# The floor of a decay scan moved into the scan, and its minimum gathered by ScalarE and taken once

## The chip, the core and the metric

The kernel runs on one core of a Trainium2 chip. A core has TensorE (PE: matrix products and transposes, with a separate track for weight loads, PEld), VectorE (DVE), ScalarE (ACT), GpSimd (POOL) and SyncE (SP, which here issues most DMAs). Each engine works through its own queue in order and waits on semaphores for what others write. The metric is the device time of the program in microseconds; smaller is better. All data is float32.

## What is computed

A gated linear recurrence (attention without softmax) for 4 batches, 8 heads, 768 positions and head width 48, then a SwiGLU block on the 3072 x 384 result:

```python
f = 1.0 / (1.0 + np.exp(-f_logit))
for t in range(S):
    state = f[:, :, t, :, None] * state + np.einsum('bhd,bhe->bhde', k[:, :, t], v[:, :, t])
    y[:, :, t] = np.einsum('bhd,bhde->bhe', q[:, :, t], state)
x = y.transpose(0, 2, 1, 3).reshape(B * S, H * D)
g = x @ w_gate
out = (g * (1.0 / (1.0 + np.exp(-g))) * (x @ w_val)) @ w_out
```

`q`, `k`, `v` and `f_logit` are (4, 8, 768, 48); `w_gate` and `w_val` are 384 x 1536, `w_out` is 1536 x 384. The entries of `f_logit` are drawn around 2.0 with a deviation of 0.5.

## The kernel before

**Chunks and units.** The sequence is cut into 6 chunks of 128 positions. A unit is one chunk `c` of one batch `b`, numbered `u = 4 * c + b`, so there are 24 units, 0 to 23. Within a unit the 8 heads lie as 4 pairs: partitions 0 to 47 and 64 to 111 hold the 48 channels of the two heads of a pair, and the free axis holds 4 pairs times 129 positions (one position ahead of each chunk, `N1 = C + 1`), 516 elements.

**What a unit does** (`attention`, a generator whose `yield`s let other work be put between its steps). Its gates come through a sigmoid on ScalarE into `gate` (by PE transposes in chunks 0 and 1, L563, by a VectorE transpose of 32 x 32 squares later, L566). A first scan on VectorE (L577) runs backward over the positions and forms `tail`, the product of the gates behind each position. Element 1 of each pair's row is then the product over the whole chunk, `whole`. Three small VectorE instructions follow, each on 128 x 4 elements: `least` is updated with the minimum of itself and `whole` (L580); `start` gets the larger of `whole` and `LEAST = 2^-60` (L581); `start` becomes its reciprocal (L582). The keys are multiplied by `tail` (`kT`, L587). A second scan (L601) runs forward from `start`, which gives the inverse products that the queries are multiplied with (`qT`, L607). TensorE forms the scores of 8 heads from `kT` and `qT` (L620) and, in most units, turns `kT` back (L624); ScalarE copies that to `kt` (L631), and VectorE applies the causal mask to the scores (`A`, L633). `decayed` is the old state times `whole` (L541). Then come the outputs `y` (L654 to L694) and the new state (`dS`, L699, L706, L708).

**The short path and the check on it.** The division by `whole` is sound only if no product over a chunk falls below `LEAST`. So the whole computation above is a short path, and `judge` looks at `least` once, near the end: a minimum over its elements on VectorE (L1317), a transpose on TensorE (L1320), a minimum over the partitions that hold channels (L1322), and a comparison with `LEAST` (L1324). The flag is loaded into registers (L1326), and only where it is set is a general path run after it (L1331). `judge` runs in the last chunk's block of the second part, after the last unit's scans.

**Staging and order.** Chunk 0's four units come first, woven together by hand. Then chunk 0's SwiGLU is done in a plain form (`mlp_plain`) together with chunk 1's units (32 to about 148 us in the profile), while the weights, which arrive as pairs of 32-bit words, are put together by ScalarE (`up`, `top`: L462, L464) and VectorE (L470 to L476). From chunk 1's SwiGLU on, the products with the three weights use schemes with fewer multiplications and more additions (`mlp_fifteen`, `down_seven`): TensorE's products (L959, L1058, L1121) are copied out by ScalarE (`c`, `aside`: L964) or added by VectorE (L860, L863), followed by silu on ScalarE (L975) and a product on VectorE (L911). The units of chunks 2 to 5 are put between these products at times written out as a table (`CHAINS`, `SCORES`, `times`).

For chunk 0 with the start of chunk 1, and for everything from about 148 us on, the order of each engine's instructions is fixed as the program writes it (`in_order`, L1226 and L1288). Between them, in the stretch of `mlp_plain`, the order is left to the scheduler of the language, but for the sums of weights.

**Buffers.** Chunks 0 and 1 alternate between two tiles `gates0/1` and two `tails0/1`; later chunks all use `gates0` and `tails0`, so a unit's first scan writes the tile that the unit before it has read. `ones` is a constant tile, 1 at the first position of each pair's row and 0 elsewhere: as the scan's second operand it starts each pair's product anew. Its memory, read as bfloat16, also feeds a few idle matmuls at the start (`keep_warm`). `least` is one 128 x 4 tile, filled with 1.0 at the start (L370).

Of the kernel before, what the change touches and what calls it, by code (L numbers as in the profile page):

```python
# [9 lines left out]
FP32 = mybir.dt.float32  # L10
# [3 lines left out]
ALU = mybir.AluOpType  # L14

LEAST = 2.0 ** -60
# [273 lines left out]
def short_path(ctx, tc, ident, least, judge, q, k, v, f_logit, moe_w_gate, moe_w_val, moe_w_out, out):  # L290
# [9 lines left out]
    nc = tc.nc  # L300
# [3 lines left out]
    HP = H // 2  # L304
# [6 lines left out]
    N1 = C + 1  # L311
# [6 lines left out]
    const = ctx.enter_context(tc.tile_pool(name="const", bufs=1))  # L318
# [29 lines left out]
    tails = [(first_pool if i else const).tile([128, HP * N1 + 2], FP32, tag=f"tails{i}", name=f"tails{i}")  # L348
             for i in range(NROT)]
    start = const.tile([128, HP * N1], FP32, tag="start", name="start")  # L350
    ones = const.tile([128, HP * N1], FP32, tag="ones", name="ones")
    nc.vector.memset(ones, 0.0)
    nc.vector.memset(ones.rearrange("p (a t) -> p a t", t=N1)[:, :, 0:1], 1.0)

    def keep_warm(n):


        p = fps.tile([128, 512], FP32, tag="m", name="idle")
        some = ones.bitcast(mybir.dt.bfloat16)
        for _ in range(n):  # L360
            nc.tensor.matmul(p, lhsT=some[:, 0:128], rhs=some[:, 0:512], start=True, stop=True)

    def pairs(t, off=0):
        return t[:, off:off + HP * N1].rearrange("p (a t) -> p a t", t=N1)
# [2 lines left out]
        nc.vector.memset(t, 0.0)  # L367
    for t in tails:
        nc.vector.memset(t, 1.0)
    nc.vector.memset(least, 1.0)  # L370

    spare = const.tile([128, 1], FP32, tag="spare", name="spare")
    nc.gpsimd.memset(spare, 0.0)
# [144 lines left out]
    def bank(name):  # L518
        return banks[-1].tile([128, 512], FP32, tag="a", name=name)
# [10 lines left out]
    def attention(u):  # L530
# [3 lines left out]
        gate, tail = (x[u % NROT if c < SQUARES else 0] for x in (gates, tails))  # L534
# [14 lines left out]
        def transposed(name, src):  # L549
            p = bank(name)  # L550
            for a in range(HP):
                nc.tensor.transpose(p[:, a * C:(a + 1) * C],
                                    src[:, 2 * a:2 * a + 2, :].rearrange("t r d -> t (r d)"), ident)
            return p.rearrange("p (a t) -> p a t", t=C)
# [6 lines left out]
        else:  # L561
            p = transposed("fTp", fr)
# [9 lines left out]
        if c >= SQUARES:  # L572
# [1 line left out]
        yield  # L574

        n = HP * N1
        nc.vector.tensor_tensor_scan(tail[:, 0:n][:, ::-1], gate[:, 0:n][:, ::-1], ones[:, ::-1], 1.0,  # L577
                                     op0=ALU.mult, op1=ALU.add)
        whole = pairs(tail)[:, :, 1:2]
        nc.vector.tensor_tensor(least, least, whole.rearrange("p a t -> p (a t)"), ALU.min)  # L580
        nc.vector.tensor_single_scalar(pairs(start)[:, :, 0:1], whole, LEAST, op=ALU.max)  # L581
        nc.vector.reciprocal(pairs(start)[:, :, 0:1], pairs(start)[:, :, 0:1])  # L582
        yield
        if c < SQUARES:
            kp = transposed("kTp", kr)
# [35 lines left out]
        if c < NCH - 1 and not turned:  # L621
            p = bank("kt")
            for a in range(HP):
                nc.tensor.transpose(p[:, a * C:(a + 1) * C], kT[:, a, :], ident)  # L624
        yield
        if c < NCH - 1:
            kt = att.tile([128, HP * C], FP32, tag="kt", name="kt")
            if turned:
                nc.sync.dma_start(out=kt, in_=turn.rearrange("t i a r e -> i t (a r e)"))
            else:  # L630
                nc.scalar.copy(kt, p)  # L631
# [10 lines left out]
        if c and b < B - 1:  # L642
# [8 lines left out]
            for a in range(HP):  # L651
                for par in range(2):
                    r = rows_of(par)
                    nc.tensor.matmul(place(a, par), lhsT=decayed[r, a, :], rhs=qT[r, a, :],  # L654
                                     start=a < 2, stop=False, skip_group_check=True)
            for par in range(2):
                for a in range(HP):
                    nc.tensor.matmul(place(a, par), lhsT=v_[:, 2 * a + par, :], rhs=A[:, par, a, :],  # L658
                                     start=False, stop=a >= HP - 2, skip_group_check=True)
# [3 lines left out]
            for h in range(H):  # L663
                a, par = h // 2, h % 2
                f = h * D
                while f < (h + 1) * D:
                    n = min((h + 1) * D, (f // 128 + 1) * 128) - f
# [28 lines left out]
        if c < NCH - 1:  # L696
            p = bank("dS")
# [19 lines left out]
    def attention_steps(c):  # L717

        runs = [attention(c * B + b) for b in range(B)]
        parts = [3, 6, 3, 3]  # L720
        order = sorted((2 * b + s, b, n) for b in range(B) for s, n in enumerate(parts))
        return [lambda b=b, n=n: [next(runs[b]) for _ in range(n)] for _, b, n in order]
# [104 lines left out]
    whole = NJ * TRIPLE + 7 * DOWN  # L827
# [339 lines left out]
    load(0, "v")  # L1167
    mark = traced[-1]
    keep_warm(5)
    first = [attention(b) for b in range(B)]  # L1170
    done = [0] * B

# [18 lines left out]
    for b in range(1, B):  # L1191
        if b == 1:
            run(1, 0)
            keep_warm(6)
        run(b, 1)
        run(b - 1, 3)
        run(b, 2)
        load_ahead(b)
        if b + 1 < B:
            run(b + 1, 0)  # L1200
        else:
            sizes.pop(0)()
        run(b - 1, 4)
# [51 lines left out]
    for c in range(2, NCH):  # L1255
        for b in range(B):
            run = attention(c * B + b)
            waiting += [((c - 2) * whole + t, lambda run=run: next(run)) for t in times(c)[b]]
# [32 lines left out]
@with_exitstack  # L1291
def kernel(
    ctx: ExitStack,
    tc: tile.TileContext,
    q: bass.AP,
    k: bass.AP,
    v: bass.AP,
    f_logit: bass.AP,
    moe_w_gate: bass.AP,
    moe_w_val: bass.AP,  # L1300
    moe_w_out: bass.AP,
    out: bass.AP,
):


    nc = tc.nc
    args = (q, k, v, f_logit, moe_w_gate, moe_w_val, moe_w_out, out)
    HP, D = q.shape[1] // 2, q.shape[3]
    flags = ctx.enter_context(tc.tile_pool(name="flags", bufs=1))
    least = flags.tile([128, HP], FP32, tag="least", name="least")  # L1310
    ident = flags.tile([128, 128], FP32, tag="idf", name="idf")
    make_identity(nc, ident)
    redo = []

    def judge(bank):
        low = flags.tile([128, 1], FP32, tag="low", name="low")
        nc.vector.tensor_reduce(low, least, axis=mybir.AxisListType.X, op=ALU.min)  # L1317
        yield
        row = bank("row")[0:1, 0:128]
        nc.tensor.transpose(row, low, ident)  # L1320
        one = flags.tile([1, 1], FP32, tag="one", name="one")
        nc.vector.tensor_reduce(one, row.rearrange("p (n d) -> p n d", n=2)[:, :, 0:D], axis=mybir.AxisListType.XY, op=ALU.min)  # L1322
        flag = flags.tile([1, 1], I32, tag="flag", name="flag")
        nc.vector.tensor_single_scalar(flag, one, LEAST, op=ALU.is_lt)  # L1324
        yield
        redo.append(nc.values_load(flag[0:1, 0:1], min_val=0, max_val=1,  # L1326
                                   skip_runtime_bounds_check_because="a comparison"))
        yield

    short_path(tc, ident, least, judge, *args)  # L1330
    with tc.If(redo[0] > 0):  # L1331
        general_path(tc, *args)
# [32 lines left out]
```

## Time and profile before

| | |
|---|---|
| device time, median of 3 runs | 612.46 us (612.24 to 613.02) |
| the profiled execution | its span, first to last instruction: 611.2 us; the page gives no time beside it |
| TensorE clock granted | 0.999 of full, mean |
| the chain that ended last, by engine | PE 67%, DVE 9%, DMA 3%, issue 3%, ACT 3%, SP queue 2% |
| first scan, L577 | 24 x 1.23 us |
| minimum, L580; maximum, L581; reciprocal, L582 | 24 each, 0.165, 0.165 and 0.180 us |
| second scan, L601 | 24 x 1.23 us |
| copies of 128 x 512 on ScalarE, L631 | 14 x 0.586 us |
| minimum in `judge`, L1317 | 0.15 us, at 536.7 us |

The profile is one execution's. A line of the page's groups or of the timeline names the source line, the engine, the operation, what is written and read, shape and count, and the busy time. A bracket at the end of a timeline line gives the idle time of the engine just before the instruction and what ended it. Durations of neighbours on VectorE and ScalarE overlap[...]. The distance between two starts therefore says better than the duration what an instruction holds its engine for.

### The profile page before, as it was taken

How to read it: one execution, taken by the hardware profiler on the slowest of the kernel's cores; microseconds unless marked ns; L12 is line 12 of the kernel's file. 1: busy time of each engine (PE TensorE's matmuls, PEld its weight loads, DVE VectorE, ACT ScalarE, POOL GpSimd, SP SyncE). 2: the span in 40 equal slices, each digit the busy share in tenths (PEclk: the TensorE clock that was granted, in tenths of full speed). 3: DMA queues.
4: the chain of work that ended last, by engine and by line, in shares of the span. 5: the costliest groups of instructions: out<-in, count | busy, mean ns of one | idle time of the engine just before them, and what ended most of it. 6: DMA issues, size and time to landing. Idle time of an engine off the chain costs nothing.

```text
span 611.2 us, 10816 instructions
## 1 busy us (share of the span) xinstructions
PE 594.2 (97%) x4036; PEld 487.9 (80%) x4036; DVE 499.2 (82%) x882; ACT 286.7 (47%) x530; POOL 7.6 (1%) x52
## 2 busy tenths in 40 slices
PE   7799999999999999999999999999999999999996
PEld 4654545566888799888899988899988899988896
DVE  7999989878999996999996889996879991566731
ACT  2465646313776522476732366742276730366600
POOL 1000000000000000000000000000000000000000
PEclk9999999999999999999999999999999999999999
DMA  9999582005323134424235344145313100100001
GB/s 149 249 213 284 174 250 79 1 14 154 89 52 69 27 95 113 118 54 96 53 95 122 104 111 111 31 114 118 105 51 90 27 6 10 53 1 2 0 1 58
DMA packets 109143, 54.10 MB, mean 89 GB/s; under 512 B 68761, under 2 KB 102169, under 8 KB 109081
## 3 DMA queue, kind: packets, MB, share of 16 engines
q1 hardware_dynamic: 107064, 50.56, 34.6%
q10 hardware_dynamic: 2016, 2.75, 1.2%
q8 instruction: 34, 0.56, 0.4%
q14 instruction: 29, 0.23, 0.1%
HBM read 44.04 MB, written 6.29 MB: 82 GB/s over the span
## 4 chain that ended last, share of the span: by engine, by line
PE 67%; DVE 9%; DMA 3%; issue 3%; ACT 3%; SPq 2%; ACTq 0%; POOL 0%; DVEq 0%; POOLq 0%
PE o L1058 15%; PE A L959 14%; PE B L959 11%; PE o L959 5%; PE o L780 5%; PE c L959 5%; PE o L1121 3%; PE sc L620 3%; PE y L658 2%; SPq L669 1%; DVE c L863 1%; PE y L679 1%; PE y L654 1%; PE dS L699 1%; DMA xT<-yT 1%
## 5 line engine op out<-in xcount | busy, mean ns | idle before, releaser
L1058 PE MATMUL o<-w_out,h 128*128 128x192 f32 x360 | 62.0, 327 | 0.5 <-DVE h L911 0.5
L959 PE MATMUL A<-xs,w_both 128*128 128x256 f32 x240 | 62.1, 381 | 0.0
L1058 PEld LDWEIGHTS o<-w_out,h 128*128 128x128 f32 x360 | 58.7, 190 | 1.7 <-DVE h L911 0.8
L964 ACT COPY c<-A 128x512 f32<-128x512 f32 x40 | 23.4, 584 | 61.3 <-PE A L959 61.3
L959 PEld LDWEIGHTS A<-xs,w_both 128*128 128x128 f32 x240 | 44.9, 190 | 6.5
L860 DVE TENSOR_TENSOR c<-c,aside 128x512 f32<-128x512 f32 x60 | 41.7, 694 | 9.8 <-ACT aside L964 8.4
L964 ACT COPY aside<-A 128x512 f32<-128x512 f32 x60 | 35.1, 586 | 30.9 <-PE A L959 30.9
L911 DVE TENSOR_TENSOR h<-h,c 128x256 f32<-128x256 f32 x100 | 41.3, 422 | 6.9 <-ACT h L975 6.8
L975 ACT ACTIVATE h<-c 128x256 f32<-128x256 f32 x100 | 39.4, 418 | 9.5 <-DVE c L860 5.8
L863 DVE TENSOR_TENSOR c<-c,aside 128x512 f32<-128x512 f32 x60 | 41.5, 692 | 2.0 <-ACT aside L964 1.7
L959 PE MATMUL B<-xs,w_both 128*128 128x256 f32 x160 | 41.2, 380 | 0.8 <-ACT aside L964 0.8
L1058 PE MATMUL o<-ws,h 128*128 128x192 f32 x240 | 41.5, 328 | 0.2 <-DVE A L633 0.2
L959 PE MATMUL c<-xT,w_both 128*128 128x256 f32 x160 | 41.2, 380 | 0.5 <-DVE c L863 0.5
L959 PE MATMUL A<-xs,extra 128*128 128x256 f32 x160 | 41.2, 380 | 0.0
L959 PE MATMUL B<-xT,extra 128*128 128x256 f32 x160 | 41.1, 379 | 0.0
L964 ACT COPY aside<-B 128x512 f32<-128x512 f32 x60 | 35.1, 586 | 11.4 <-PE B L959 6.9
L1058 PEld LDWEIGHTS o<-ws,h 128*128 128x128 f32 x240 | 39.1, 190 | 0.8 <-DVE A L633 0.4
L633 DVE TENSOR_TENSOR A<-sc,causal 128x512 f32<-128x512 f32 x48 | 30.8, 684 | 9.9 <-PE sc L620 9.8
L863 DVE TENSOR_TENSOR c<-o,c 128x512 f32<-128x512 f32 x40 | 27.8, 694 | 10.3 <-ACT h L975 5.8
L959 PEld LDWEIGHTS B<-xs,w_both 128*128 128x128 f32 x160 | 30.2, 190 | 5.2 <-ACT aside L964 1.2
L959 PEld LDWEIGHTS c<-xT,w_both 128*128 128x128 f32 x160 | 30.3, 190 | 5.0 <-DVE c L863 0.9
L959 PEld LDWEIGHTS A<-xs,extra 128*128 128x128 f32 x160 | 30.3, 190 | 4.4 <-ACT c L964 0.3
(140 smaller groups left out, 1138.8 us busy)
## 6 DMA issues: line engine op xcount, KB each, us to landing
fsquares<-in_f_logit_dram SPq DMA_DIRECT2D x64, 96.0 KB, 2.7
ksquares<-in_k_dram SPq DMA_DIRECT2D x64, 96.0 KB, 2.6
qsquares<-in_q_dram SPq DMA_DIRECT2D x64, 96.0 KB, 2.3
v<-in_v_dram SPq DMA_DIRECT2D x24, 192.0 KB, 3.2
w<-in_moe_w_gate_dram SPq DMA_DIRECT2D x6, 768.0 KB, 6.4
w<-in_moe_w_val_dram SPq DMA_DIRECT2D x6, 768.0 KB, 5.3
w<-in_moe_w_out_dram SPq DMA_DIRECT2D x6, 768.0 KB, 5.7
out_dram<-ob ACTq DMA_DIRECT2D x14, 192.0 KB, 2.3
```

What stands on the lines that cost most here:

```text
L620: nc.tensor.matmul(sc[par][:, a * C:(a + 1) * C], lhsT=kT[r, a, :], rhs=qT[r, a, :], start=True, stop=True)
L633: nc.vector.tensor_tensor(A[:, par], sc[par].rearrange("p (a t) -> p a t", t=C), causal.unsqueeze(1).broadcast_to((128, HP, C)), ALU.mult)
L658: nc.tensor.matmul(place(a, par), lhsT=v_[:, 2 * a + par, :], rhs=A[:, par, a, :], start=False, stop=a >= HP - 2, skip_group_check=True)
L780: nc.tensor.matmul(p, lhsT=hidden_tile(h, n // 2)[:, n % 2 * 2 + b // 2, b % 2 * C:(b % 2 + 1) * C], rhs=w_out[:, j, :], start=(n == 0), s ...
L860: nc.vector.tensor_tensor(dst, a, b, ALU.add)
L863: nc.vector.tensor_tensor(dst, a, b, ALU.subtract)
L911: lagging.append(lambda: f(*args))
L959: nc.tensor.matmul(p[name][:, n, :], lhsT=weights_of[a][:, n, j, :], rhs=tokens[b], start=fresh and n == 0, stop=True, skip_group_check=True)
L964: nc.scalar.copy(t, p[name])
L975: nc.scalar.activation(dst, src[:, 0, :], AF.Silu)
L1058: nc.tensor.matmul(p[:, n, :], lhsT=lhsTs[j][:, n * C:(n + 1) * C], rhs=rhs[:, j, :], start=first and j == order[0] and n == 0, stop=j == ...
L1121: nc.tensor.matmul(p, lhsT=hidden_tile(h, j)[:, 2, n * C:(n + 1) * C], rhs=b22[:, j, :], start=j == order[0], stop=j == order[-1])
```

## The change

The first scan's second operation becomes a maximum, and its second operand a tile `floor` that holds 1 at the first position of each pair's row and `LEAST` elsewhere. The gate at a pair's first position is 0, so the running value there becomes 1 as before; elsewhere a running product below `LEAST` is lifted to it. `whole` is then at least `LEAST`, and the separate maximum goes: the reciprocal is taken of `whole` directly. The running minimum goes as well. In its place ScalarE copies each unit's `whole` to a row of a larger `least` (24 rows of 4), in the step that follows the scores, ahead of the copy of `kt`. `judge` takes one minimum over all 96 elements of a partition, and its comparison becomes "at most `LEAST`", since a lifted product now equals it. The fill of `least` with 1.0 is dropped, as each row is written.

```diff
     start = const.tile([128, HP * N1], FP32, tag="start", name="start")
-    ones = const.tile([128, HP * N1], FP32, tag="ones", name="ones")
-    nc.vector.memset(ones, 0.0)
-    nc.vector.memset(ones.rearrange("p (a t) -> p a t", t=N1)[:, :, 0:1], 1.0)
+    floor = const.tile([128, HP * N1], FP32, tag="floor", name="floor")
+    nc.vector.memset(floor, LEAST)
+    nc.vector.memset(floor.rearrange("p (a t) -> p a t", t=N1)[:, :, 0:1], 1.0)
...
-        some = ones.bitcast(mybir.dt.bfloat16)
+        some = floor.bitcast(mybir.dt.bfloat16)
...
-    nc.vector.memset(least, 1.0)
...
         n = HP * N1
-        nc.vector.tensor_tensor_scan(tail[:, 0:n][:, ::-1], gate[:, 0:n][:, ::-1], ones[:, ::-1], 1.0,
-                                     op0=ALU.mult, op1=ALU.add)
+        nc.vector.tensor_tensor_scan(tail[:, 0:n][:, ::-1], gate[:, 0:n][:, ::-1], floor[:, ::-1], 1.0,
+                                     op0=ALU.mult, op1=ALU.max)
         whole = pairs(tail)[:, :, 1:2]
-        nc.vector.tensor_tensor(least, least, whole.rearrange("p a t -> p (a t)"), ALU.min)
-        nc.vector.tensor_single_scalar(pairs(start)[:, :, 0:1], whole, LEAST, op=ALU.max)
-        nc.vector.reciprocal(pairs(start)[:, :, 0:1], pairs(start)[:, :, 0:1])
+        nc.vector.reciprocal(pairs(start)[:, :, 0:1], whole)
         yield
...
         yield
+        nc.scalar.copy(least[:, u, :], whole.rearrange("p a t -> p (a t)"))
         if c < NCH - 1:
             kt = att.tile([128, HP * C], FP32, tag="kt", name="kt")
...
-    least = flags.tile([128, HP], FP32, tag="least", name="least")
+    least = flags.tile([128, q.shape[0] * q.shape[2] // 128, HP], FP32, tag="least", name="least")
...
-        nc.vector.tensor_reduce(low, least, axis=mybir.AxisListType.X, op=ALU.min)
+        nc.vector.tensor_reduce(low, least, axis=mybir.AxisListType.XY, op=ALU.min)
...
-        nc.vector.tensor_single_scalar(flag, one, LEAST, op=ALU.is_lt)
+        nc.vector.tensor_single_scalar(flag, one, LEAST, op=ALU.is_le)
```

## The prediction

> **What bounds the kernel now.** I read the page's first part, then the waits of TensorE by stretch, then the VectorE and ScalarE timelines around the lines that the change touches, and last the chain that ended last.
>
> ```profile
> PE 594.2 (97%) x4036; PEld 487.9 (80%) x4036; DVE 499.2 (82%) x882; ACT 286.7 (47%) x530; POOL 7.6 (1%) x52
> ```
>
> TensorE is busy for 97% of the span, so what VectorE saves is worth only what TensorE waits for VectorE. The waits of TensorE from 32 to 242 us, as the waits view has them (who waited for whom, total, times, longest):
>
> ```profile
> PE B L959 <- ACT aside L964: 0.8, 1, 0.8
> PE o L780 <- DVE h L771: 0.7, 1, 0.7
> PE o L1058 <- DVE h L911: 0.5, 1, 0.5
> PE c L959 <- DVE c L863: 0.5, 1, 0.5
> PE sc L620 <- DVE qT L607: 0.4, 1, 0.4
> PE o L1058 <- DVE A L633: 0.2, 1, 0.2
> ```
>
> These sum to 3.1 us. The same view from 242 to 606 us names no wait at all, and by stretch (PE busy, PEld busy, DVE busy, ...):
>
> ```profile
> 242.00:340.00 98.00, 97.91 (x729) 87.83 (x729) 86.61 (x153) 48.95 (x94) 0.84 (x5) 1.00 0.38 92
> 340.00:432.00 92.00, 92.00 (x682) 82.48 (x681) 80.11 (x142) 46.97 (x90) 0.84 (x5) 1.00 0.38 94
> 432.00:526.00 94.00, 94.00 (x632) 84.27 (x631) 71.80 (x132) 43.05 (x85) 0.74 (x4) 1.00 0.18 49
> ```
>
> There VectorE has gaps and TensorE none: units 12 to 23 (half of all) can give nothing. What one unit's first scan and the three small instructions behind it take, in the VectorE timeline (start, duration):
>
> ```profile
> 5.99 1.23 DVE L577 TENSOR_TENSOR_SCAN tails<-gates,ones 128x516 f32<-128x516 f32 x1 [1.77 <-ACT gates L563]
> 7.26 0.17 DVE L580 TENSOR_TENSOR least<-least,tails 128x4 f32<-128x4 f32 x1
> 7.34 0.16 DVE L581 TENSOR_SCALAR start<-tails 128x4 f32<-128x4 f32 x1
> 7.54 0.18 DVE L582 RECIPROCAL start<-start 128x4 f32<-128x4 f32 x1
> 7.63 0.66 DVE L587 TENSOR_TENSOR kT<-kTp,tails 128x512 f32<-128x512 f32 x1
> ```
>
> The minimum holds the engine for 0.08 us, since the independent maximum starts that much later; the reciprocal needs the maximum and starts 0.20 us behind it. With both gone the reciprocal can start at 7.26, so 0.28 us go per unit. Where other work was put between them (the fifth unit, at 43.92) less goes:
>
> ```profile
> 45.51 0.16 DVE L580 TENSOR_TENSOR least<-least,tails 128x4 f32<-128x4 f32 x1
> 45.59 0.17 DVE L581 TENSOR_SCALAR start<-tails 128x4 f32<-128x4 f32 x1
> 45.66 0.68 DVE L771 TENSOR_TENSOR h<-h,val 128x512 f32<-128x512 f32 x1
> ```
>
> Here the pair costs 0.15 us.
>
> [...] a scan of 516 elements takes 1228 ns (L577) where a plain two-operand instruction on 512 takes 681 (L633). [...] The nearest row here:
>
> ```profile
> L560 ACT ACTIVATE spare<-spare 128x1 f32<-128x1 f32 x4 | 0.8, 204 | 0.0
> ```
>
> So 0.20 us for the new 128x4 copy. The 128x512 copies (0.59 us) follow each other at 0.48 us, an overlap of 0.11, so the copy should hold ScalarE for about 0.09 us (estimate). [...] the page of the kernel has table loads only at L557, L560, L563, L767 and L975 (sigmoid and silu), so I charge no load.
>
> **The change part by part.**
>
> Scan with maximum in place of addition, 24 times. The trace doesn't show this form. [...] I take 1.23, unchanged[...].
>
> Minimum and maximum removed, 24 of each. On VectorE: 24 x 0.28 = 6.7 us at most. What of it reaches the end:
> - Units 0 to 3 (0 to 32 us): nothing. TensorE waits at 20.35 us for the load of the fourth fraw, which comes through a queue that is issuing without a pause from 0.8 us; the earlier savings end there. From there the path runs PE y, dS, sc, then VectorE's mask at 23.73 us, which itself waited 0.29 us for PE sc, so that unit 3's saving turns into a longer wait. Behind the mask no removed instruction stands.
> - Units 4 to 7 (32 to 148 us): VectorE is busy 43.3 of 46 us and then 60.2 of 70, alternating with ScalarE over the weight pieces. Unit 4's 0.15 comes off the 0.4 us wait of sc at 49.34. Unit 6's 0.14 (95.91 to 96.05) comes off the 0.7 us wait at 108.96, since VectorE has no gap from 90.98 to there. Unit 5's 0.15 I count as lost in the ScalarE waits at 76.93, 83.16 and 90.98. Unit 7's 0.14 works on sc at 128.16, which the chain shows starting 0.12 us after qT released it: 0.1.
> - Units 8 to 11 (148 to 242 us): unit 8's 0.28 works on sc at 160.09, released by qT as well: about 0.2, what the spacing of TensorE's starts is above usual there. Unit 9's is lost at 179.17, where VectorE waits 0.79 us for PE sc. Unit 10's (186.79) counts in full, because VectorE has no gap from 181 to 209 us and the waits at 194.43, 201.21 and 210.76 are its lag: 0.28. Unit 11's scan is at 219.08, behind the last such wait but the 0.2 of L633, which itself waits for TensorE: nothing.
> Sum: 0.15 + 0.14 + 0.1 + 0.2 + 0.28 = 0.87 us.
>
> The copy on ScalarE, 24 x 0.09 = 2.2 us of an engine with 47% work. It stands directly ahead of the kt copy of L631, or of the next thing where there is none. For units 0 to 3 ScalarE idles 3.13, 1.96, 1.40 and 1.40 us just there: hidden. For unit 9 there is no cover:
>
> ```profile
> 180.63 0.59 ACT L964 COPY c<-A 128x512 f32<-128x512 f32 x1 [2.41 <-PE A L959]
> 181.11 0.59 ACT L631 COPY kt<-kt 128x512 f32<-128x512 f32 x1
> 181.59 0.61 ACT L964 COPY c<-B 128x512 f32<-128x512 f32 x1
> ```
>
> Behind them are a table load and the silu of 183.51 (ends 183.93), and VectorE's L911 takes that at 184.00. 0.09 later makes VectorE lose some 0.06 in its stretch without gaps. From 242 us on no TensorE instruction waits, so a copy shifted by 0.09 is covered by the gaps of ScalarE. Charge: 0.1 us. Bounds: 0, and 8 units x 0.20 = 1.6 if the overlap failed and nothing hid it before 242 us.
>
> The new waits. The copy waits for the scan, which in the fixed order lies several VectorE instructions back. The next scan into the same tail waits for the copy; queued behind it on VectorE are the reciprocal, the kT product and all later additions. The closest pair is unit 8's copy at about 164.95 (ends 165.15) and unit 9's scan at 166.59: 1.4 us of cover; unit 12 to 13 has 2.3 us. Nothing.
>
> Judging once over 128x96 in place of 128x4: 0.15 us plus 92 x 1.02 ns (from (681 - 165) / 508) is 0.24, once, at 536.7 us, where TensorE doesn't wait. The last copy comes before the mask of unit 23 at 502 us. The memsets: the new fill is the old one with another value, one of 0.06 us goes at 4.16, ahead of a 1.77 us wait. The test for equality as well can't start the other path: sigmoid of 2.0 is 0.88, and 128 of these give about 2^-24, far from 2^-60. Nothing for all of these.
>
> Net: 0.87 - 0.1, say 0.8 us. The profiled span is 611.2; it becomes 610.4. The median of the runs shown, 612.46, lies 1.3 us above the span, for start and end around it, which the change doesn't touch: 611.7 us.
>
> **The rivals.**
> 1. Nothing arrives: TensorE's six waits are each taken over by the next releaser (a weight transfer, as ScalarE waits 2.1 us for one at 51.69, or an ACT copy). For it: VectorE and ScalarE alternate there, and only one is shortened. Against: VectorE runs without a gap into four of the waits. 612.4 us.
> 2. More than counted: in 32 to 148 us the order isn't written out, and other work filling in differently may remove both of the 1.1 us of waits there, and half of the 1.8 of 194 to 211 us, with 0.2 at 160: 612.46 - 2.2 = 610.3 us. All six waits would be 3.1 (609.4), the ceiling; the full 6.7 us of VectorE can't come through.
> 3. Slower: the new copy blocks ScalarE's queue in 32 to 148 us. It is ready as soon as the scan is, its place there isn't fixed, and if it is put directly behind the scan's planned time, while VectorE really runs late, ScalarE stands still with up, top and silu behind it, for which VectorE's joins and TensorE's banks wait. Read off: unit 6's scan ends at 95.41 and ScalarE starts an up at 94.85 (0.56 lost), unit 5's ends at 65.92 against a top at 65.60 (0.32). Placed one ScalarE instruction earlier, each adds about 0.9. Three or four units give 0.9 to 3.3 us; with 2.5 the net is +1.7: 614.2 us. It decides from 2.0 us of stall on (0.8 to eat up, 1.2 to be seen). Against: ScalarE has gaps of 3 to 5 us in the stretch.
>
> **How the numbers follow.** Forecast 0.5 (611.7, own range 611.1 to 612.3), rival 1 0.1, rival 2 0.16, rival 3 with a slower scan 0.24. About 0.2%, 1.2 us, is what a measurement of this kernel can tell from no change. Faster than 611.2: rival 2 and 0.06 of the forecast, 0.22. Slower than 613.7: rival 3, 0.24 less what of it stays small, and as much again for an order that turns out worse without it, 0.24. Same: 0.54. The range reaches to rivals 2 and 3: 610.3 to 614.2.
>
> **What would show it.** Right: L582 starting 0.04 us behind the end of L577, a scan of 1.23 us, the copies at about 0.2 us with no table load, the wait of L780 near 0.5 to 0.6, the VectorE-bound waits of 194 to 211 us some 0.2 smaller in sum, still no TensorE wait after 242 us. Wrong: an ACT copy with idle time ended by DVE tails ahead of it, a scan of another length, a different order of the joins between 32 and 148 us with a longer wait of TensorE there, or a scan waiting for ACT.

## The result and the profile after

| | before | after |
|---|---|---|
| device time, median | 612.54 us (612.24 to 613.03, 6 runs) | 610.27 us (609.45 to 611.44, 6 runs) |
| span of the profiled execution | 611.2 us | 609.6 us (its time: 611.44 us) |
| last TensorE instruction starts at | 605.11 us | 603.85 us |
| VectorE busy | 499.2 us, 882 instructions | 494.3 us, 833 instructions |

The ratio after to before is 0.9956, 95% interval 0.9943 to 0.9968: faster by 2.3 us, where 0.8 was forecast, and just outside the range. The first line of the page of after answers to the busy line of before that the prediction shows:

```profile
PE 595.8 (98%) x4036; PEld 491.1 (81%) x4036; DVE 494.3 (81%) x833; ACT 288.5 (47%) x554; POOL 7.6 (1%) x52
```

The first unit on VectorE, in the timeline of after (start, duration, the operation, then idle time in brackets; line numbers after are up to three smaller than before):

```profile
5.93 1.23 DVE L576 TENSOR_TENSOR_SCAN tails<-gates,floor 128x516 f32<-128x516 f32 x1 [1.72 <-ACT gates L562]
7.20 0.18 DVE L579 RECIPROCAL start<-tails 128x4 f32<-128x4 f32 x1
7.30 0.66 DVE L584 TENSOR_TENSOR kT<-kTp,tails 128x512 f32<-128x512 f32 x1
```

This is as forecast: the scan with a maximum takes the same 1.23 us, the reciprocal starts 0.04 us behind it, and kT starts 0.33 us earlier than before (7.63), of which 0.06 is the earlier scan. The view of the tile `least` shows the ScalarE copy and the one minimum of the end, also as priced (forecast 0.20 and 0.24 us):

```profile
L623 ACT COPY least<-tails x24: 180/200/211, 8.3 to 500.2; 128x4 f32<-128x4 f32 x24
L1315 DVE TENSOR_REDUCE low<-least x1: 242/242/242, 535.4 to 535.4; 128x1 f32<-128x96 f32 x1
```

So the prices were right, and yet the gain is nearly three times the forecast. Most of it is found where the prediction had put nothing. TensorE's waits from 0 to 32 us, before:

```profile
PE fTp L552 <- DMA fraw<-in_f_logit_dram: 2.3, 2, 1.8
PE idle L361 <- DVE ones L353: 2.1, 1, 2.1
PE sc L620 <- DVE qT L607: 1.5, 2, 0.8
```

and after:

```profile
PE idle L361 <- DVE floor L353: 2.1, 1, 2.1
PE sc L617 <- DVE qT L604: 1.8, 2, 1.0
PE y L677 <- ACT kt L629: 0.7, 1, 0.7
```

The wait for the load of `fraw` is gone, and the scores of unit 3 start 2.20 us earlier (27.60 to 25.40). The table by stretch, from 4 to 14 us, points to the reason in its last two columns (share of the DMA engines, packets that overlap counted each, and GB/s); before:

```profile
4.00:14.00 10.00, 8.18 (x71) 5.72 (x73) 7.99 (x17) 2.07 (x4) 0.11 (x1) 1.00 1.48 165
```

and after:

```profile
4.00:14.00 10.00, 9.02 (x87) 7.23 (x86) 8.08 (x12) 2.47 (x5) 0.10 (x1) 1.00 1.05 221
```

The same loads, issued by the same queue, run at 221 GB/s in place of 165. From about 11 us on the faster stretch also carries pieces of the weights in longer rows; from 4 to 11 us, where both move short rows alone, it is 215 against 166. No instruction of the change touches them. What it does touch is where they land: `least` is allocated early, and its growth from 16 to 384 bytes per partition moves every tile that is allocated behind it by 352 bytes (the 16 had taken 32). No trace shows an address; in the allocation of the built programs the tiles `fraw`, `kraw`, `qraw` and two of the four `v` tiles lie 160 bytes behind a multiple of 256 before, and at a multiple of 256 after. Their rows are 192 bytes long with a stride of 256, so that before every row that the DMA writes lies across a multiple of 256, and after none does.

From 32 to 242 us the waits of TensorE after are:

```profile
PE sc L617 <- DVE qT L604: 0.8, 1, 0.8
PE B L957 <- ACT aside L962: 0.6, 1, 0.6
PE o L1056 <- DVE h L909: 0.5, 1, 0.5
PE c L957 <- DVE c L861: 0.5, 1, 0.5
PE y L677 <- ACT diagonal L546: 0.3, 1, 0.3
PE o L1056 <- DVE A L631: 0.2, 1, 0.2
```

The waits of L780 (0.7 us) and of sc at 49.34 are gone, B is 0.2 shorter. Weights queue behind the first loads, and a wait of ScalarE for one of them, which the kernel before has, is gone too:

```profile
51.69 0.92 ACT L462 ACTIVATE up<-w 128x768 int32<-128x768 uint32 x1 [2.11 <-DMA w<-in_moe_w_val_dram]
```

In the kernel after the same instruction starts at 48.83, without such a wait. Two waits of TensorE are new: sc waits 0.8 us for qT (at 126.5 us, unit 7), and y waits for `diagonal`. One more thing in this execution isn't of the change: TensorE's granted clock stood at 0.5 from 28.0 to 31.4 us, and the lead of TensorE over the kernel before fell from 2.20 us at unit 3 to 0.85 behind it (the first products with val start at 34.18 against 35.03). The second profile of the same kernel below has no such stretch (1.00 from 22 to 32 us).

### The profile page after: what moved, and what is told of

Same layout as the page of the kernel before. It is cut to its first block, busy times and chain, and to the rows that moved or that the text cites. A ratio compares the mean times of both kernels' runs of the same rounds, so it can differ in the third digit from the quotient of the medians.

```text
span 609.6 us, 10796 instructions
## 1 busy us (share of the span) xinstructions
PE 595.8 (98%) x4036; PEld 491.1 (81%) x4036; DVE 494.3 (81%) x833; ACT 288.5 (47%) x554; POOL 7.6 (1%) x52
## 4 chain that ended last, share of the span: by engine, by line
PE 85%; DVE 10%; SPq 1%; issue 1%; DMA 1%; ACT 1%; POOL 0%; DVEq 0%; ACTq 0%; POOLq 0%
PE o L1056 17%; PE A L957 15%; PE B L957 12%; PE gate L755 5%; PE val L755 5%; PE o L957 5%; PE c L957 5%; PE sc L617 4%; PE o L778 3%; PE o L1119 3%; PE y L677 2%; PE y L656 2%; PE dS L697 2%; PE y L652 1%; DVE c L861 1%
```

## The experiments

Two theories were set against each other. **Placement:** the loads are faster because of where the tiles lie, and the instructions add little. **Instructions:** the saved VectorE time is the gain, and the loads follow from it. Each run has its own runs of the kernel before on the same chip; ratios are with those. Times of one kernel scatter by 1 us and more, but positions in its trace hardly do: where no load is waited for, kernels that differ only in something later start the scores of the same unit within 0.06 us of each other, most within 0.02. So the small steps are read from positions, each from one profiled execution; "lead" is how much earlier an instruction starts than in the kernel compared with.

**The kernel before with the tiles placed as after** ("the placed kernel before"). Nothing else changes.

```diff
-    least = flags.tile([128, HP], FP32, tag="least", name="least")
+    least = flags.tile([128, 96], FP32, tag="least", name="least")[:, 0:HP]
```

> The kernel before with its row of minima allocated as 384 bytes, as after, and otherwise unchanged: all later SBUF tiles move by 352 bytes, from 160 to 0 bytes past a multiple of 256. Placement theory: the first loads land as in the kernel after (the second qraw near 8.4 us instead of 10.1, some 210 GB/s in place of 163 between 4 and 14 us), the wait for fraw near 20 us is gone, 610.7 to 611.6 us, ratio near 0.9975. Instruction theory (the gain comes from the two VectorE instructions gone): the loads and the time stay as before, 612.5 us, ratio 1.000.

Measured: 610.11 us (609.64 to 611.03), ratio 0.9952 (0.9939 to 0.9965); 243 GB/s:

```profile
4.00:14.00 10.00, 7.89 (x75) 6.02 (x78) 8.05 (x17) 2.12 (x4) 0.10 (x1) 1.00 1.08 243
```

One allocation, without one instruction of the change, brings the whole gain, and more than the placement theory had put on it (0.9975). Its lead over the kernel before grows in steps: 1.33 us at unit 3, 1.64 at unit 4, 2.64 at unit 6, 2.92 at the end. The first step is the wait for `fraw`. The one at unit 6 goes with the weights: SP issues the piece that ScalarE had waited for at 41.29 us in place of 46.02, ScalarE starts on it at 48.14 without a wait, and TensorE's waits for sc at 49.34 and for L780 are gone, though VectorE has as many instructions as before.

**The kernel after with the tiles displaced as before.**

```diff
-    least = flags.tile([128, q.shape[0] * q.shape[2] // 128, HP], FP32, tag="least", name="least")
+    least = flags.tile([128, 34, HP], FP32, tag="least", name="least")[:, 0:q.shape[0] * q.shape[2] // 128, :]
```

> The kernel after with its tile of products allocated 160 bytes larger, so that the later tiles lie 160 bytes past a multiple of 256 as in the kernel before. Placement theory: the loads are slow again (163 GB/s from 4 to 14 us), 611.4 to 611.9 us, ratio near 0.9985: what the forecast's sum for VectorE gave. Instruction theory: 610.3 us as after, ratio 0.996.

Measured: 613.5 us (612.75 to 614.46), ratio 1.0006 (0.9998 to 1.0014). The whole instruction change, at the old place, is worth nothing that can be measured; 611.4 to 611.9 us was expected of the placement theory. The wait for `fraw` is back, and 0.7 us longer, about what the units ahead of it had gained, just as the prediction said of these units:

```profile
PE fTp L551 <- DMA fraw<-in_f_logit_dram: 3.0, 2, 2.5
```

**The kernel after once more**, unchanged, on the same chip.

> The kernel after once more, beside the others on the same chip. Both theories: 609.4 to 611.4 us, ratio 0.994 to 0.997, with more spread between runs than before; the slower runs are those in which TensorE's granted clock falls to half for 3.4 us near 28 us.

Measured: 609.83 us (609.53 to 610.04), ratio 0.9943 (0.993 to 0.9956), 242 GB/s. The wider spread that was expected isn't there.

**Which property of the place counts.** Two more sizes of `least` in the kernel before: 64 bytes, which puts the load tiles 192 bytes behind a multiple of 256 (a multiple of 64, but each row crosses), and 160 bytes, which puts them 32 behind (not a multiple of 64, but no row crosses).

```diff
-    least = flags.tile([128, HP], FP32, tag="least", name="least")
+    least = flags.tile([128, 16], FP32, tag="least", name="least")[:, 0:HP]
```

> The kernel before with its row of minima allocated 32 bytes larger: later tiles lie 192 bytes past a multiple of 256, so a multiple of 64, but the 192-byte rows of the loads still cross a multiple of 256. If the crossing of 256 bytes is what costs: loads as slow as before, 612.5 us. If the 64-byte alignment is: loads as fast as after, 611 us.

Measured: 611.94 us (610.33 to 614.58), ratio 0.999 (0.998 to 0.9999), hardly faster than before, and the slow rate:

```profile
4.00:14.00 10.00, 8.51 (x75) 6.13 (x78) 8.05 (x17) 2.12 (x4) 0.11 (x1) 1.00 1.49 166
```

```diff
-    least = flags.tile([128, HP], FP32, tag="least", name="least")
+    least = flags.tile([128, 40], FP32, tag="least", name="least")[:, 0:HP]
```

> The kernel before, `least` stretched so that the load tiles begin 32 bytes behind a multiple of 256: each row of 192 bytes then lies within one block of 256 bytes, but does not begin on a multiple of 64 or 256. If the crossing of a 256-byte boundary is the cost, the first loads run near the fast rate (230 to 245 GB/s from 4 to 14 us, against 165), the wait of TensorE for the load of fraw is gone, and the time is 610.1 to 610.6 us. If the beginning of a row decides, the rate stays near 165 and the time near 612.5.

Measured: 610.88 us (610.56 to 611.72), ratio 0.996 (0.9946 to 0.9974), and the fast rate:

```profile
4.00:14.00 10.00, 8.05 (x75) 6.13 (x78) 8.05 (x17) 2.12 (x4) 0.10 (x1) 1.00 1.06 226
```

For the rate of the loads, crossing a multiple of 256 bytes is what costs: from 4 to 14 us it is 165 and 166 GB/s where the rows cross (160 and 192 bytes behind), and 243 and 226 where none does (0 and 32), all in the kernel before. Up to unit 11 the run at 32 bytes and the one at 0 agree within 0.01 us at the first scores of each unit. The time at 32 bytes lies 0.3 us above what was expected; its profiled execution (611.72 us, the slowest of the five) loses 1.03 us between units 11 and 12, a place that comes back below.

The rate isn't all of the gain, though. The run at 192 bytes has the slow rate and the wait for `fraw` (2.5 us), and yet leads the kernel before by 1.17 us at unit 6 and by 0.72 at the end: ScalarE's wait for the weight is 0.55 us there in place of 2.11. Why that weight comes earlier at 192 bytes than at 160 no run shows.

**The two halves of the change, each alone, at the good place.** First the maximum in the scan, with the minimum left on VectorE (`floor`, the scan and `is_le` as in the change):

```diff
         whole = pairs(tail)[:, :, 1:2]
         nc.vector.tensor_tensor(least, least, whole.rearrange("p a t -> p (a t)"), ALU.min)
-        nc.vector.tensor_single_scalar(pairs(start)[:, :, 0:1], whole, LEAST, op=ALU.max)
-        nc.vector.reciprocal(pairs(start)[:, :, 0:1], pairs(start)[:, :, 0:1])
+        nc.vector.reciprocal(pairs(start)[:, :, 0:1], whole)
```

> The kernel before with the load tiles placed as after and the maximum folded into the scan; the minimum stays on VectorE. Against the placed kernel before (610.1 us, first scores of unit 3 at 26.27, of unit 7 at 125.52, last TensorE instruction at 602.19): if the reciprocal's wait for the maximum is what the change saves (0.20 us a unit), the first scores of unit 3 come 0.5 to 0.8 us earlier, the reciprocal starts 0.08 us behind the minimum, and the time is 609.5 to 610.0. If instructions are worth nothing at equal placement, nothing moves by over 0.3 us.

Then the minimum by ScalarE, with `ones`, the addition in the scan and the maximum on VectorE:

```diff
         whole = pairs(tail)[:, :, 1:2]
-        nc.vector.tensor_tensor(least, least, whole.rearrange("p a t -> p (a t)"), ALU.min)
         nc.vector.tensor_single_scalar(pairs(start)[:, :, 0:1], whole, LEAST, op=ALU.max)
...
+        nc.scalar.copy(least[:, u, :], whole.rearrange("p a t -> p (a t)"))
```

> The minimum gathered by ScalarE alone; the maximum stays on VectorE, the load tiles lie as after. The minimum held VectorE for 0.08 us a unit, so at most 0.2 us by unit 3. If the copy queued behind the scan on ScalarE costs something in the stretch from 32 to 148 us, the first scores of unit 7 come later than in the placed kernel before (125.52) and the time is 610.2 to 611; if not, 609.9 to 610.1.

Measured: 609.03 us (608.49 to 612.05), ratio 0.9946 (0.9928 to 0.9963), and 610.17 us (609.62 to 611.25), ratio 0.9951 (0.9937 to 0.9965). The intervals overlap with each other and with that of the placed kernel before (0.9939 to 0.9965), so the times part none of the three; the traces do, as far as one execution of each goes. Starts of the first scores of some units and of the last TensorE instruction, as differences in us from the placed kernel before (all at a place where no row crosses, and minus is earlier; the last three columns are the runs that follow):

| | placed before, at | after again | maximum alone | minimum alone | after, order kept | after, order and queue | maximum and queue |
|---|---|---|---|---|---|---|---|
| unit 3 | 26.27 | -0.86 | -0.78 | -0.30 | -0.87 | -0.86 | -0.77 |
| unit 4 | 47.71 | -1.03 | -0.95 | -0.39 | -1.04 | -1.03 | -0.95 |
| unit 6 | 107.17 | -1.03 | -0.88 | -0.39 | -1.04 | -1.03 | -0.94 |
| unit 7 | 125.52 | -0.37 | -1.02 | -0.47 | -1.22 | -1.21 | -1.08 |
| unit 8 | 157.49 | -0.60 | -1.21 | -0.54 | -1.46 | -1.45 | -1.27 |
| unit 11 | 223.27 | -0.70 | -1.42 | -0.43 | -1.56 | -1.55 | -1.46 |
| unit 12 | 244.41 | -0.69 | -0.68 | +0.20 | -0.80 | -1.61 | -1.52 |
| last | 602.19 | -0.47 | -0.88 | -0.04 | -0.72 | -1.94 | -1.58 |

With the loads out of the way, units 0 to 3 do give something: 0.86 us for the change, 0.78 for the maximum alone. The maximum carries most of the lead up to unit 11. The ScalarE copies cost TensorE nothing that this table shows. From 0 to 32 us the view of waits has TensorE once behind a copy, for 0.5 us, where it stood 0.5 us behind the copy of `state` in the placed kernel before. And ScalarE of the kernel after stands idle for 2.65 us before one of them,

```profile
42.68 0.20 ACT L623 COPY least<-tails 128x4 f32<-128x4 f32 x1 [2.65 <-DVE tails L576]
```

which is the mechanism of the third rival, without a cost at unit 4: at this place ScalarE of the placed kernel before idles too, for 4.17 us up to 45.07. The change loses its lead elsewhere: 0.66 us between units 6 and 7.

**The order of unit 7.** In the stretch whose order the scheduler chooses, it chose otherwise. VectorE's timeline around unit 7 in the placed kernel before:

```profile
124.09 0.68 DVE L587 TENSOR_TENSOR kT<-kTp,tails 128x512 f32<-128x512 f32 x1
124.70 0.68 DVE L607 TENSOR_TENSOR qT<-qTp,gates 128x512 f32<-128x512 f32 x1
125.29 0.95 DVE L474 SCALAR_TENSOR_TENSOR top<-w,top 128x768 int32<-128x768 int32 x1
```

and in the second profile of after:

```profile
122.86 0.95 DVE L473 SCALAR_TENSOR_TENSOR top<-w,top 128x768 int32<-128x768 int32 x1
123.73 0.68 DVE L584 TENSOR_TENSOR kT<-kTp,tails 128x512 f32<-128x512 f32 x1
124.33 0.68 DVE L604 TENSOR_TENSOR qT<-qTp,gates 128x512 f32<-128x512 f32 x1
```

The join of a weight now stands ahead of kT and qT, and holds them for 0.87 us (122.86 to 123.73). The edit makes it follow qT (in `join`, `queries` holding unit 7's qT product):

```diff
                 nc.vector.scalar_tensor_tensor(top[:, i], hi[:, i], -(1 << 30), top[:, i], op0=ALU.bitwise_and,
                                                op1=ALU.bitwise_or)
+                if queries:
+                    keep_order([queries[0], traced[-1]])
```

> The kernel after with one pair of VectorE instructions the other way round: the join's 128x768 instruction (0.95 us) behind the kT and qT products of unit 7 in place of ahead of them, as in the kernel before. If that order cost what the saved instructions had gained, TensorE's wait of 0.8 us for qT near 125 to 126 us falls to 0.2 or less, and the time is 0.4 to 0.6 us below the kernel after: 609.2 to 609.5 us. If TensorE meets the same delay later (a weight that is joined later), a new wait of about 0.5 us appears behind it and the time stays at 609.8.

Measured: 609.05 us (608.72 to 610.27), ratio 0.9933 (0.9918 to 0.9948). The wait for qT is gone from the list, and unit 7 comes 0.86 us earlier than in the kernel after (125.16 to 124.30). But the lead of 1.56 us at unit 11 is 0.80 at unit 12, with a wait of TensorE as the sign of it ("order kept" names this run below):

```profile
PE y L681 <- ACT diagonal L548: 0.4, 1, 0.4
```

**The same at the old place**, where the prediction's sum was made.

> The kernel after with the load tiles put back where they lay before (160 bytes behind a multiple of 256) and the order of unit 7 on VectorE kept as before. This is the case that the prediction had in mind. Its sum then says: first scores of unit 7 about 0.3 us ahead of the kernel before (128.16), of unit 12 about 0.7 to 0.8 ahead (247.49), time 0.7 to 0.9 us below the kernel before. If the saved instructions are worth nothing on the path, unit 12 stays within 0.2 us of before.

Measured: 612.67 us (611.6 to 614.69), ratio 0.9997 (0.9986 to 1.0007). Differences from the kernel before:

| | before, at | after displaced | the same, order kept |
|---|---|---|---|
| unit 1 | 15.73 | -0.50 | -0.47 |
| unit 3 | 27.60 | +0.05 | +0.11 |
| unit 4 | 49.34 | -0.42 | -0.37 |
| unit 6 | 109.81 | -0.10 | -0.24 |
| unit 7 | 128.16 | +0.56 | -0.43 |
| unit 8 | 160.09 | +0.36 | -0.64 |
| unit 11 | 225.88 | +0.25 | -0.73 |
| unit 12 | 247.49 | +0.13 | -0.43 |
| last | 605.11 | -0.04 | -0.51 |

Up to unit 11 the lead is close to the forecast sum, 0.73 us of 0.77. Unit 12 was expected at 0.7 to 0.8 and has 0.43: the same place as in the run before. The time, expected 0.7 to 0.9 us below the kernel before, can't be told from it.

**What takes the lead at unit 12.** `diagonal` shares its tile with `yT`, so its fill on POOL waits until the transfers xT<-yT have read that. In the run with the order kept, on POOL and on SP's queue:

```profile
233.20 0.42 POOL L546 MEMSET diagonal<- 128x384 f32 x1 [13.12 <-DMA xT<-yT]
```

```profile
223.19 1.80 SPq L428 DMA_DIRECT2D qsquares<-in_q_dram  x4
225.09 6.72 SPq L671 DMA_DIRECT2D xT<-yT  x10
```

SP issues ten small transfers in 6.7 us, behind three groups of loads. Unit 12 follows that fill: in nine traces in which SP issues all of these transfers, the kernel before among them, its first scores start 10.42 us behind the fill (10.41 to 10.43), whatever lead unit 11 has. How far VectorE is ahead hardly moves the fill: it is at 233.31 us in the second run of the kernel after and at 233.20 with the order kept, where unit 11 comes 0.85 us earlier. The edit gives every second head's transfer to POOL, in the third unit of each later chunk:

```diff
-                    nc.sync.dma_start(out=xT[c][f % 128:f % 128 + n, f // 128, b * C:(b + 1) * C],
+                    queue = nc.gpsimd if c >= SQUARES and b == B - 2 and h % 2 else nc.sync
+                    queue.dma_start(out=xT[c][f % 128:f % 128 + n, f // 128, b * C:(b + 1) * C],
```

It was put on the kernel after with the order kept, and on the kernel with the maximum alone:

> The kernel after with the order of unit 7 kept and half of the transfers xT<-yT of the third unit of each later chunk issued by POOL in place of SP. In the run with the order alone the lead of 1.56 us at unit 11 falls to 0.80 at unit 12, where TensorE waits 0.4 us for `diagonal`, whose memset waits on POOL for those transfers, of which SP issues one each 0.67 us. If SP's rate of issue is this next limit, the memset comes over 2 us earlier, the wait for `diagonal` is gone, the lead at unit 12 is 1.4 to 1.6 us, and the time 608.3 to 608.6 us. If issuing on POOL is slow or disturbs VectorE, the memset comes no earlier and VectorE's stretch grows: 609 us or more.

> The placed kernel before with the maximum folded into the scan, the minimum kept on VectorE, and half of those transfers issued by POOL. Against the same without POOL's transfers (lead of 1.42 us at unit 11, 0.68 at unit 12): if SP's issue is the limit there, the lead at unit 12 stays at 1.3 to 1.4 us and the time is 608.3 to 608.6 us; otherwise 609.

Measured: 608.93 us (607.96 to 609.66), ratio 0.9933 (0.9919 to 0.9947), and 609.04 us (608.45 to 609.13), ratio 0.993 (0.9916 to 0.9943). In the first one, on POOL:

```profile
222.06 2.62 POOL L672 DMA_DIRECT2D xT<-yT  x5 [1.96 <-ACT least L627]
230.59 0.42 POOL L546 MEMSET diagonal<- 128x384 f32 x1 [5.91 <-DMA xT<-yT]
```

The fill comes 2.6 us earlier, the wait for `diagonal` is gone, the first scores of unit 12 now start 12.2 us behind the fill (12.6 in the second run), and the lead at unit 12 is 1.61 us (1.52): SP's issue was the limit there. The distance of 10.42 us also accounts for the loss of the run at 32 bytes, whose fill is at 235.03 us against 234.00 in the placed kernel before; what moves SP by that much between two runs of the same instructions stays open. In the times this is not to be told from the order alone (609.05 on another chip, with equal ratios), and both medians miss the expected 608.3 to 608.6. These medians of about 609 us are, with those of the order alone and of the maximum alone, the shortest of the study, 0.8 below the second run of the kernel after, but their intervals overlap with its own (0.993 to 0.9956).

## Why the prediction was wrong

**The step that failed is one that isn't in it.** The part-by-part working prices the larger `least` only as an operand (the minimum over 128x96, 0.24 us), not as an allocation. Its effect on all later tiles was not considered, and it is the gain: 2.8 us for the allocation alone (ratio 0.9952), 2.3 for the whole change (0.9956). The term of the sum that it overturns is "Units 0 to 3 (0 to 32 us): nothing", which measured 2.20 us at unit 3: 1.33 are in the placed kernel before, and 0.86 come from the instructions once the load no longer holds TensorE. With it falls the sentence on units 0 to 3, that TensorE waits for a load "which comes through a queue that is issuing without a pause" and "the earlier savings end there". That reading was right for the kernel before, and the run at the old place shows it to the word: half a microsecond gained at unit 1 is gone at unit 3. But it took the rate of the loads for given, and with it the wait of 2.1 us for a weight at 51.69. The number was in sight: 165 GB/s from 4 to 14 us with the DMA engines 90% busy or more in each of 40 slices, on loads that the kernel is waiting for. A rate that bounds a stage has to be asked what sets it, and whether the change touches that.

**The sum of 0.87 less 0.1 came out in its own case, in part by luck.** At the old place and in the old order, by unit 11: 0.73 us. Term by term (forecast, measured in that run as the change of the lead): unit 4 0.15, 0.47 (the wait of sc went altogether; mis-sized, and 0.28 of it is in the run at 192 bytes too, where no instruction was saved); unit 6 0.14, while its lead at unit 6 is 0.13 smaller than at unit 4 (0.24 against 0.37), so that it brought nothing and some was lost, though the weight at 51.69 came 0.53 us earlier; unit 7 0.1, 0.19; unit 8 0.2, 0.21; unit 9 nothing, 0.10 lost; unit 10 0.28, 0.19 (of TensorE's waits from 194 to 211 us only that of B shrank, from 0.75 to 0.56 us; the other two, 0.5 each, stayed). Units 0 to 3, at nothing, came out 0.11 late. So the terms of units 4 and 6 carry errors of 0.3, of opposite sign, and the sum owes its closeness to that. And at unit 12 only 0.43 is left.

**The order was named and not priced.** "A different order of the joins between 32 and 148 us with a longer wait of TensorE there" stood among the signs of being wrong and had a share of the chance of slower, but no price. It happened, at about 0.85 us between units 6 and 7 at either place: at unit 7 the two runs at the old place stand at +0.56 and -0.43, with 0.14 between them at unit 6 already. Together with the limit at unit 12 it is why the instruction change is worth nothing at the old place (ratio 1.0006): with the order kept, 0.51 us of lead reach the end in the trace, and without, 0.04.

**What is late next** was sought on VectorE, ScalarE and TensorE. SP's issue of the small transfers was left out, and takes 0.3 us at the old place and 0.8 at the new one with the order kept. In the kernel before only the weight loads ahead of the products y show it, from 32 to 242 us:

```profile
PEld y L679 <- ACT diagonal L547: 0.6, 2, 0.4
```

The waits of TensorE's products, which the prediction summed, do not name it, and yet unit 12 stands 10.42 us behind the fill there too. A saving ahead of unit 12 counts only as far as the fill moves with it.

**Right:** the scan's 1.23 us (the author's estimate, as no trace had shown this form), the reciprocal 0.04 us behind it, copies of 0.20 us without a table load (30 table loads in either trace, for the same five operations), no cost of the ScalarE copies on the path that shows (0.1 was charged), no TensorE wait from 242 us on (the view names none). The rival "more than counted" gave the right time, 610.3 us, by a wrong mechanism, which is luck: it wanted both waits of 32 to 148 us gone by another filling-in, and half of the 1.8 us of 194 to 211. The two are gone, but in the placed kernel before, where no instruction was saved and the weights come earlier, they are gone as well; of the 1.8 us, 1.6 are still there. At a good place the instructions do bring more than counted, 1.61 us at unit 12 in the trace, but only with the order and SP's queue set right as well, and the times don't tell this from the placed kernel before with certainty (0.9919 to 0.9947 against 0.9939 to 0.9965). One reading was off without weight: the 1.3 us between the median and the span compares two executions; in every run on record time and span of the same execution lie 1.7 to 1.9 us apart.

Left open: why the scheduler chose the other order, why the weight comes earlier at 192 bytes, what moves SP ahead of unit 12, and what brought the low clock from 28.0 us in one of two profiles of the same kernel. It stood at 0.50 from 28.00 to 31.41 us there; no trace shows the cause.

## What to carry to other kernels

A change of a tile's size is also a change of every address behind it. Before pricing an edit's instructions, compare the two allocations, and where a DMA writes short rows, see whether each lies within one block of 256 bytes: with rows of 192 bytes that gave 215 to 227 GB/s here, against 166 to 168 where they crossed. And where two kernels differ by an allocation, measure the allocation alone before crediting the instructions; here it was one line and the whole gain. And ask of a saving not only which wait it shortens, but what the next stage waits for that the saving doesn't move.

## What the runs showed of the hardware

Loads of 192-byte rows into on-chip memory ran at 166 to 168 GB/s where each row crosses a multiple of 256 bytes (160 and 192 bytes behind it), and at 215 to 227 GB/s where none does (0 and 32 behind it), from 4 to 11 us in seven traces; the 221 to 243 of the tables up to 14 us have some weights in them. Among rows that cross, and among rows that don't, where they begin made no difference that shows: 221 and 221 GB/s in the kernel before at 0 and 32, 166 and 167 at 160 and 192. Why a row that crosses takes longer no trace shows. From the share and the packets of the DMA view between 4 and 11 us, a packet takes 1.47 x 16 x 7 us / 6145 = 27 ns in the kernel before, and 1.09 x 16 x 7 us / 7962 = 15 ns in the kernel after (estimates).

A transfer issued on POOL held that engine for 0.52 us (2.62 us for five, with the order kept and the queue changed); one on SP's queue took 0.67 us (6.72 for ten, with the order kept). A scan of 516 elements took 1225 ns with a maximum as its second operation and 1228 with an addition.
